# RWKV recurrence and feed-forward network in one kernel: state products in the mixing step, chunk 0 loaded in longer packets, new order tables

## The chip, the cores and the metric

The kernel runs on one core of a Trainium2 chip. The core has a matrix engine (TensorE, PE in the profile; its weight loads are listed as PEld), a vector engine (VectorE, DVE), an engine for activation functions (ScalarE, ACT), a general engine (GpSimd, POOL), and a synchronisation engine (SyncE, SP), which here issues nearly all DMAs. The engines run side by side, each through its own list of instructions in order, and wait for each other through semaphores. SBUF is the working memory of 128 partitions, PSUM the memory of eight banks into which TensorE writes. The metric is the time of one execution in microseconds, lower is better.

## The reference

For every batch entry b (4) and head h (8), a state matrix of 48 x 48 runs over 768 time steps; then all results go through a feed-forward network with a squared ReLU.

```python
B, H, S, D = r.shape                       # 4, 8, 768, 48
state = zeros((B, H, D, D))
for t in range(S):
    kt, vt, rt, wt = k[:, :, t], v[:, :, t], r[:, :, t], w[:, :, t]
    cur = einsum('bhd,bhe->bhde', u[None] * kt, vt)
    y[:, :, t] = einsum('bhd,bhde->bhe', rt, state + cur)
    state = wt[..., None] * state + einsum('bhd,bhe->bhde', kt, vt)
x = y.transpose(0, 2, 1, 3).reshape(B * S, H * D)     # 3072 x 384
h = maximum(x @ w_in, 0)                              # w_in 384 x 2048
out = (h * h) @ w_out                                 # w_out 2048 x 384
```

All arrays are fp32. The decays w lie between 0.80 and 0.95.

## The kernel before

**Units and chunks.** Time is cut into six chunks of 128 steps. One *unit* is one chunk c of one batch entry b, all eight heads; there are 24 units. Two heads share the partitions: head 2p stands on partitions 0 to 47, head 2p + 1 on 64 to 111 (J = 64, HP = 112), with p from 0 to 3 along the columns. Within a unit the recurrence becomes matrix products:

1. w, k and r of a unit arrive with time on the partitions (tile st). For chunks 1 to 5, DVE transposes blocks of 32 (L438) and 16 small DMAs spread them (L448), so that heads and channels stand on the partitions (tile pt). For chunk 0, TensorE does it: *turn* (L468), four transposes per tensor, into PSUM banks that are still free.
2. DVE forms the running products of w (scan, L484). ACT takes logarithm and exponential for the inverse (L491, L492), DVE multiplies: r~ = r times decay (rt, L495), and k~ by one Newton step (kn, L501, L502, L504).
3. beta is minus the sum over channels of r k u: two products on POOL (rk, L511, L513) and a sum on DVE (L514). ACT puts beta on the diagonals of two tiles Ms (diag, L521).
4. TensorE forms the scores of k~ and r~ (L532) into two banks, DVE copies the causal part over the diagonal tiles (mask, L536).
5. TensorE turns k~ back to time on the partitions (ktok, L544), ACT copies it to SBUF as Kt (L546).
6. The *mixing* step: products of the state with r~ (inter, L564) and of Ms with v (part, L572), in PSUM. ACT and DVE write the result as the feed-forward network's input x, in two fp32r parts hi and lo (L604, L605). In chunk 0, which has no state yet, the pair SPLIT is brought to its place by a copy ly and selection products (L586); later, small DMAs from tile x3 do that (L612).
7. The *state products* Kt with v (outer, L624): a step of its own with a bank of its own, then DVE adds them to the state (L632) and POOL multiplies by the decay of the chunk (L633). In chunk 0 DVE does the one product that is needed (L630). Chunk 5 needs none.

**Feed-forward.** The 2048 hidden columns are 16 steps f of 128. One step on the 512 columns of a chunk (4 batch entries x 128 steps of time) is: nine products into a bank hp (first, L653; three input tiles, each hi x hi, lo x hi, hi x lo), ReLU on ACT (L658), square on DVE (L659), hi part on ACT (L661), lo part on DVE (L662), then three products per batch entry that accumulate over all f in the banks ob0 to ob3 (second, L668). HALF = (6, 16, 0, ...) says that the first 6 steps of chunk 0 and all of chunk 1 run in two halves of two batch entries. The results leave through ACT copies and SP DMAs (L678, L682). For the last chunk, b = 1 and 3 are copied by DVE and go out through SP's queue, b = 0 and 2 by ACT through ACT's; b = 3 is copied half by DVE, half by ACT (L676, L680).

**Weights.** Both weight matrices arrive raw in eight groups g (two steps f each) and are split once into hi and lo parts in SBUF: two passes on ACT, three on DVE and one on POOL for each matrix of a group (split_w, L381). This lies beside chunks 0 and 1.

**PSUM.** Of the eight banks four are the accumulators ob, two are the pool hp and two the pool a. Scores, k~ turned back, mixing and state products all draw from the two a banks.

**What sets the order.** Every step is added to a planner (class Plan) with its engine, an estimated cost, a rank, and what it reads and writes. The planner runs a list schedule over estimated times (constants LAT, QUEUES, START, ...), takes among the steps that could start first the one of the lowest rank, hands out the tiles of the pools, and so writes one fixed order of instructions for each engine. The ranks come from the tables in class Ranks: one offset per kind of step, for chunk 0 (AT0), chunk 1 (AT1) and the others (AT), and for the weights and the feed-forward network. While PE would idle in the first 110 us by the plan, it gets *filler* transposes of the identity (L186, L712), which compute nothing. PE executes in this order: a step that is not ready holds up all behind it.

Of the kernel before, what the change touches and what calls it, by code (L numbers as in the profile page):

```python
# [35 lines left out]
class Plan:  # L36
# [156 lines left out]
class Ranks:  # L193
    AT = {'load': -139.75, 'z': 137.75, 'pt': -192, 'rk': -68, 'beta': -95.75, 'far': 178.75, 'v': 86, 'scan': 126.75, 'ln': -6.25, 'rt': -60.5, 'kn': 68.25, 'diag': -6.5, 'mt': -217.25, 'mask': 121.25, 'ktp': -306, 'kt': 263.5, 'mix': -111.5, 'x': 42.5, 'x3': -127.75, 'send': -288.5, 'dS': -95.75, 'S': -108.5}
    AT0 = {'load': -191.75, 'turn': -44.5, 'rk': 202.25, 'beta': -96, 'far': 179.75, 'v': -119, 'scan': -62, 'ln': 22, 'rt': -197.25, 'kn': -247.25, 'diag': -59.75, 'mt': -160.25, 'mask': -55.25, 'ktp': -67.75, 'kt': -39.75, 'mix': -207.25, 'x': -15.5, 'x3': -445.5, 'send': -140.25, 'dS': -172.75, 'S': -20.75}
    AT1 = {'load': -18.75, 'z': 292.25, 'pt': -54.25, 'rk': 265.5, 'beta': 219.25, 'far': 46.25, 'v': 45.75, 'scan': -1.25, 'ln': -41.5, 'rt': -120.5, 'kn': 3.25, 'diag': 57.75, 'mt': 3.5, 'mask': -138.5, 'ktp': 58, 'kt': 35, 'mix': -180.25, 'x': -185.5, 'x3': -144.25, 'send': -255.25, 'dS': -175.5, 'S': 98.75}
    U0 = (-54.25, -18, 58.5, 12)
    C1 = (5.5, 8.75, 72.25, 68.25)
    W0 = (-158.25, -38, -18.25, -1.25, 2.75, 4, 10, 16.25)
    WL = (17.5, -93.75, -2.75, -6.5, -3.75, 0.5, 9.25, 9)  # L200
    OFF = {'hp': 133.5, 'g': -8.25, 'ob': 69.5, 'os': 306}
    LAG = 74.5
# [18 lines left out]
RANKS = Ranks()  # L221
# [6 lines left out]
def kernel(  # L228
# [81 lines left out]
    st0 = [place(f"st0{i}", [128, 3, 2, H, J], F32, a) for i, a in enumerate((placed[f"ri{NG - 1}"], placed["x1"]))]  # L310
    for t in st0:
        V.memset(t[:, :, :, :, D:J], 1.0)
# [10 lines left out]
    P.pool("st0", [t.rearrange("s t b h x -> s (t b h x)") for t in st0])  # L323
# [92 lines left out]
    def attention(c, b, rank):  # L416
# [45 lines left out]
        if c == 0:  # L462
            home = (["o0", "o1", "o2"], ["o3", "hp", "hp"], ["o2", "o3", "a"], ["o2", "o3", "a"])[b]
            ps = {}
            for i, h in zip((0, 2, 1), (home[0], home[2], home[1])):
                ps[i] = Slot(h) if h in ("hp", "a") else ("ob", int(h[1]))

                def turn(i=i):  # L468
                    to = tl(ps[i]).rearrange("a (p s) -> a p s", p=NP)
                    pairs = st.tile.rearrange("s (t b p x) -> s t b p x", t=3, b=2, p=NP)[:, i, ui]  # L470
                    for p in range(NP):
                        T.transpose(out=to[:, p], in_=pairs[:, p], identity=ident)
# [119 lines left out]
        else:  # L592
# [3 lines left out]
            if ui == 0:  # L596
                d["x3"] = Slot("x3", n)
# [212 lines left out]
```

## Time and profile before

| | us |
|---|---|
| timed runs | 547.17, 552.87, 2872.64 (median 552.87) |
| profiled execution | 546.83 |
| its span, first to last instruction | 545.1 |
| PE busy / DVE / ACT / POOL | 525.9 / 361.2 / 289.9 / 103.0 |
| mean granted TensorE clock | 0.996 |

The profile gives for each engine the time in which an instruction of it was running. The sum over engines is far above the span because they overlap; what matters is which engine the others wait for in a given stretch. Busy PE time is an upper bound: matmuls are pipelined and their ends are modelled. "L653" is line 653 of the kernel printed above; "hp<-x,wi" says what is written and what is read; "SPq" and "ACTq" are issues of DMAs on those engines' queues; "in_w_dram" is an input in main memory.

### The profile page before, as it was taken

Reading aid. Unit: us, or ns where it says so; the run is one execution under the profiler, and the core shown is the slowest. Engines: PE = TensorE matmul, PEld = TensorE weight load, DVE = VectorE, ACT = ScalarE, POOL = GpSimd, SP = SyncE. Lnnn points to the kernel's source line nnn. Section 1 sums busy time; section 2 is a strip of 40 time slices with the busy share of each in tenths; the row PEclk is TensorE's granted clock in tenths of the full one; section 3 lists DMA queues with packets and bytes.
Section 4 is the critical chain, followed back from the end, with each engine's and each line's share of the span. In section 5 each row is a group of like instructions: output and inputs, shape, how many; then the busy total and the mean of one; then the engine's idle time right before and its main releaser. Section 6 shows DMA issues by size and latency. Waiting matters only on the chain.

```text
span 545.1 us, 10409 instructions
## 1 busy us (share of the span) xinstructions
PE 525.9 (96%) x3920; PEld 462.0 (85%) x3920; DVE 361.2 (66%) x672; ACT 289.9 (53%) x696; POOL 103.0 (19%) x119
## 2 busy tenths in 40 slices
PE   7888999999999999999999999999999999999994
PEld 6767988879999898888888888888888989999894
DVE  6899989989678595958779495976643233233241
ACT  2769886674854747466474756645333223233231
POOL 5344644532302020021202102020000000000000
PEclk9999999999999999999999999999999999999998
DMA  9999989158592776878375695954011000010001
GB/s 167 207 248 248 206 190 215 29 84 137 79 155 51 100 120 92 123 87 158 50 108 68 93 153 71 160 72 49 1 43 45 2 0 1 0 59 1 0 1 63
DMA packets 206584, 50.89 MB, mean 93 GB/s; under 512 B 196288, under 2 KB 201408, under 8 KB 206528
## 3 DMA queue, kind: packets, MB, share of 16 engines
q1 hardware_dynamic: 206096, 49.57, 52.7%
q8 instruction: 33, 0.54, 0.5%
q10 hardware_dynamic: 432, 0.59, 0.3%
q14 instruction: 23, 0.19, 0.1%
HBM read 31.65 MB, written 4.72 MB: 67 GB/s over the span
## 4 chain that ended last, share of the span: by engine, by line
PE 75%; DVE 7%; DMA 6%; SPq 5%; ACT 4%; issue 1%; DVEq 0%
PE hp L653 32%; PE ob L668 31%; PE a L572 4%; PE a L532 3%; DMA ri<-in_moe_w_in_dram 2%; SPq L429 2%; SPq L448 2%; PE a L564 2%; DMA st<-in_w_dram 1%; PE a L624 1%; ACT m L521 1%; PE a L544 1%; DVE st L438 1%; DMA v<-in_v_dram 1%; DVE g L662 1%
## 5 line engine op out<-in xcount | busy, mean ns | idle before, releaser
L653 PE MATMUL hp<-x,wi 128*128 128x512 f32 (+1 forms) x1062 | 220.5, 356 | 2.0 <-DVE g L662 1.8
L668 PE MATMUL ob<-wo,g 128*128 128x384 f32 x1152 | 221.4, 339 | 0.0
L668 PEld LDWEIGHTS ob<-wo,g 128*128 128x128 f32 x1152 | 198.5, 188 | 7.1 <-issue 2.0
L653 PEld LDWEIGHTS hp<-x,wi 128*128 128x128 f32 x1062 | 173.3, 188 | 32.7 <-DVE g L662 4.5
L658 ACT ACTIVATE t<-hp 128x512 f32<-128x512 f32 (+1 forms) x118 | 61.2, 519 | 119.8 <-PE ob L668 103.5
L659 DVE SCALAR_TENSOR_TENSOR hp<-hp,t 128x512 f32<-128x512 f32 (+1 forms) x118 | 70.1, 595 | 81.9 <-ACT t L658 80.8
L662 DVE TENSOR_TENSOR g<-hp,g 128x512 fp32r<-128x512 f32 (+1 forms) x118 | 68.8, 584 | 33.7 <-ACT g L661 31.7
L661 ACT CAST g<-hp 128x512 fp32r<-128x512 f32 (+1 forms) x118 | 59.6, 506 | 54.3 <-DVE hp L659 54.1
L521 ACT ACTIVATE m<-ident,beta 128x128 f32<-128x128 f32 x192 | 60.8, 393 | 5.0 <-DVE beta L514 4.8
L605 DVE SCALAR_TENSOR_TENSOR x<-a,x 112x128 fp32r<-112x128 f32 (+2 forms) x64 | 20.1, 344 | 31.4 <-ACT x L604 29.4
L511 POOL TENSOR_TENSOR st<-st 128x384 f32<-128x384 f32 x24 | 25.0, 1041 | 63.6 <-DVE st L438 62.5
L536 DVE COPY_PREDICATED m<-caus,a 128x512 f32<-128x512 uint8 x48 | 34.2, 731 | 4.1 <-PE a L532 4.1
L484 DVE TENSOR_TENSOR_SCAN pt<-pt,zero 112x128 f32<-112x128 f32 x80 | 29.6, 411 | 5.6 <-DMA x<-x 2.9
L572 PE MATMUL a<-m,v 128*48 128x128 f32 (+1 forms) x384 | 27.5, 278 | 1.9 <-DVE m L536 1.9
L532 PEld LDWEIGHTS a<-pt 48*128 48x128 f32 x384 | 23.6, 187 | 6.1 <-issue 2.7
L604 ACT ACTIVATE x<-a 112x128 fp32r<-112x128 f32 (+2 forms) x64 | 18.1, 322 | 19.6 <-PE a L572 18.1
L532 PE MATMUL a<-pt 48*128 48x128 f32 x384 | 28.2, 285 | 0.2
L491 ACT ACTIVATE m<-pt 112x512 f32<-112x512 f32 x24 | 15.2, 633 | 24.6 <-DVE pt L484 20.5
L438 DVE STREAM_TRANSPOSE st<-st 128x1152 f32<-128x1152 f32 x20 | 27.0, 1359 | 0.0
L513 POOL TENSOR_TENSOR st<-st,un 128x384 f32<-128x384 f32 x24 | 26.6, 1112 | 1.8
L572 PEld LDWEIGHTS a<-m,v 128*48 128x48 f32 (+1 forms) x384 | 20.2, 128 | 6.9 <-issue 4.4
L410 POOL TENSOR_TENSOR wi<-q,wi 128x768 fp32r<-128x768 f32 x8 | 16.1, 2018 | 43.3 <-ACT wi L409 24.3
(81 smaller groups left out, 394.9 us busy)
## 6 DMA issues: line engine op xcount, KB each, us to landing
pt<-st SPq DMA_DIRECT2D x80, 96.0 KB, 3.0
ro<-in_moe_w_out_dram SPq DMA_DIRECT2D x8, 768.0 KB, 6.6
v<-in_v_dram SPq DMA_DIRECT2D x24, 192.0 KB, 5.6
st<-in_w_dram SPq DMA_DIRECT2D x11, 384.0 KB, 4.2
st<-in_k_dram SPq DMA_DIRECT2D x11, 384.0 KB, 5.7
st<-in_r_dram SPq DMA_DIRECT2D x11, 384.0 KB, 6.4
pt<-st SPq DMA_DIRECT2D x80, 48.0 KB, 3.4
out_dram<-q SPq DMA_DIRECT2D x20, 192.0 KB, 3.2
```

The source lines that it names most:

```text
L438: V.transpose(out=zt[:, i].rearrange("a t p q i -> a t (p q) i"), in_=sv[:, :, i].rearrange("s t p q x -> s t (p q) x"))
L484: lambda p=p: V.tensor_tensor_scan(out=pt[:, 0, p], data0=src(0)[:, p], data1=zero.broadcast_to([HP, C]), initial=1.0, op0=ALU.mult, op1=A ...
L521: A.activation(mv(j)[:, p], ident, AF.Copy, scale=beta.tile[:, 2 * p + j:2 * p + j + 1])
L532: T.matmul(mts[j].tile.rearrange("s (p t) -> s p t", p=NP)[:, p], pt[js, 2, p], pt[js, 1, p], start=True, stop=True)
L536: lambda j=j: V.copy_predicated(out=mv(j), mask=caus.unsqueeze(1).broadcast_to([128, NP, C]), data=mts[j].tile.rearrange("s (p t) -> s p t ...
L572: T.matmul(spot(p)[to:to + n + D], vt.tile[:, o - n:o + D], mv(j)[:, p], start=(c == 0 and p == SPLIT), stop=True, skip_group_check=True)
L653: T.matmul(hp.tile[:, 0:n], wi[f][:, wl, kt], xT[:, kt, xl, xs], start=(m == 0), stop=(m == 3 * KT - 1))
L658: P.add("act", 0.5 if full else 0.28, rank("g"), lambda: A.activation(t(), h(), AF.Relu), r=[hp], w=[(g, 1)])
L659: P.add("dve", 0.61 if full else 0.33, rank("g"), lambda: V.scalar_tensor_tensor(out=h(), in0=h(), scalar=0.0, in1=t(), op0=ALU.max, op1=A ...
L661: P.add("act", 0.53 if full else 0.31, rank("g"), lambda: A.copy(out=hi(), in_=h()), r=[hp], w=[(g, 0)])
L662: P.add("dve", 0.61 if full else 0.33, rank("g"), lambda: V.tensor_tensor(out=lo(), in0=h(), in1=hi().bitcast(F32), op=ALU.subtract), r=[h ...
L668: T.matmul(obs[b][:, 0:DM], g.tile[0][:, gl, o:o + C], wo[f][:, wl], start=(f == 0 and m == 0), stop=(f == NF - 1 and m == 2))
```

## The change

- **State products.** For chunks 1 to 4, outer is called at the end of the mixing step and writes into columns 256 to 447 of the bank yb that holds two pairs of the mixing result. The step of its own and its bank are gone; the mixing step now also waits for Kt, and yb is kept until DVE has updated the state. In chunk 0 it stays a step of its own.
- **Loads of chunk 0.** w, k and r of each unit of chunk 0 come with (head, block of eight time steps) on the 128 partitions and 8 x 48 values, 1,536 bytes, in a row, one DMA per tensor and unit (12 instead of 9). The turn becomes 16 matmuls against columns of the identity, eight time steps by two heads of a pair, each writing 4 x 16 columns with a stride of eight.
- **r k u in chunk 0.** ACT writes -k into k~'s place, DVE multiplies it by r, and four small products with a column form of u (tile ut, made at the start from two small loads, a transpose and two copies) give beta in the bank that held w; ACT copies it out. The load of the row form of u goes from ACT's queue to SP's, after chunk 0's loads.
- **Squares of chunk 0.** ACT instead of DVE squares the ReLU result.
- **Last results.** All four go out on ACT's queue; b = 3 is copied by ACT in one piece, b = 1 still by DVE.
- **Planner.** New latencies, start and idle constants, some new costs, and new numbers in all rank tables.

The diff, cut to its core (the rank tables, all of which change, are left out but for one line):

```diff
-    LAT = {"pe": 0.2, "act": 0.1, "dve": 0.1, "pool": 0.1}
+    LAT = {"pe": 0.24, "act": 0.14, "dve": 0.14, "pool": 0.15}
...
-    LANES, RUNS, SLACK, START = 8, 2300, 2.0, 2.4
+    LANES, RUNS, SLACK, START = 8, 2300, 2.0, 1.4
...
-    IDLE = (110.0, 4.0, 0.3, 0.12)
+    IDLE = (110.0, 2.8, 0.3, 0.12)
...
-    OFF = {'hp': 133.5, 'g': -8.25, 'ob': 69.5, 'os': 306}
+    OFF = {'hp': 5.25, 'g': -342.5, 'ob': 16.25, 'os': -244}
...
-    st0 = [place(f"st0{i}", [128, 3, 2, H, J], F32, a) ...
+    TB = C // 16
+    st0 = [place(f"st0{i}", [128, 3, 2, TB * D + PC], F32, a) ...
     for t in st0:
-        V.memset(t[:, :, :, :, D:J], 1.0)
+        V.memset(t[:, :, :, TB * D:], 1.0)
+    ut = at.tile([HP, NP, 2], F32, name="ut")
+    V.memset(ut, 0.0)
...
-    nc.scalar.dma_start(out=un, in_=u.rearrange("h d -> (h d)").partition_broadcast(128))
-    G.tensor_scalar(out=un, in0=un, scalar1=-1.0, scalar2=None, op0=ALU.mult)
+    u8 = P.pools["m"][1][1][0:H, 0:HP]
+    V.memset(u8, 0.0)
+    for j in range(2):
+        nc.scalar.dma_start(out=u8[:, j * J:j * J + D], in_=u)
+    us = Slot("hp")
+    P.add("pe", 0.1, -300, lambda: T.transpose(out=us.tile[0:HP, 0:H], in_=u8, identity=ident[0:H, 0:H]), w=[us])
+    def columns():
+        for j in range(2):
+            js = slice(j * J, j * J + D)
+            A.copy(out=ut[js, :, j], in_=us.tile[js, j:H:2])
+    P.add("act", 0.3, -300, columns, r=[us], w=["ut"])
+    P.add("sp", 0.7, RANKS.unit(0, 3, "load") + 0.5, lambda: nc.sync.dma_start(out=un, ...
+    P.add("pool", 1.0, RANKS.unit(0, 3, "load") + 0.5, lambda: G.tensor_scalar(out=un, ...
...
-            for b0, m in ((b, 1), (b + 1, 1)) if (c, b) == (0, 0) else ((b, 2),):
+            for b0 in (b, b + 1) if c == 0 else ():
+                for i, src in ((0, w), (2, k), (1, r)):
+                    def load(i=i, src=src, b0=b0):
+                        nc.sync.dma_start(out=st.tile.rearrange("s (t b x) -> s t b x", t=3, b=2)[:, i, b0 - b, 0:TB * D],
+                                          in_=src[b0, :, ss, :].rearrange("h (a s) d -> h a (s d)", s=TB))
+                    P.add("sp", 0.65, rank("load") + b0 - b, load, w=[(st, b0 - b, i)], after=after, runs=128)
+            for b0, m in ((b, 2),) if c else ():
...
-                    to = tl(ps[i]).rearrange("a (p s) -> a p s", p=NP)
-                    pairs = st.tile.rearrange("s (t b p x) -> s t b p x", t=3, b=2, p=NP)[:, i, ui]
-                    for p in range(NP):
-                        T.transpose(out=to[:, p], in_=pairs[:, p], identity=ident)
-                P.add("pe", 0.5, rank("turn"), turn, r=[(st, ui, i)], w=[ps[i]])
+                    to = tl(ps[i]).rearrange("a (p x y) -> a p x y", p=NP, y=TB)
+                    rows = st.tile.rearrange("s (t b x) -> s t b x", t=3, b=2)[:, i, ui]
+                    pick = ident.rearrange("s (p j x) -> s p j x", p=NP, j=2)
+                    for y in range(TB):
+                        for j in range(2):
+                            n = (J, D)[j]
+                            T.matmul(to[j * J:j * J + n, :, :, y], rows[:, y * D:y * D + n], pick[:, :, j], start=True, stop=True, ...
+                P.add("pe", 1.0, rank("turn"), turn, r=[(st, ui, i)], w=[ps[i]], mode=3)
...
+        beta = Slot("beta")
+        if c == 0:
+            P.add("act", 0.53, rank("rk"), lambda: A.activation(pt[:, 2], src(2), AF.Copy, scale=-1.0), r=keys(2), w=[PT[2]])
+            P.add("dve", 0.62, rank("rk"), lambda: V.tensor_tensor(out=pt[:, 2], in0=pt[:, 2], in1=src(1), op=ALU.mult), r=keys(1), w=[PT[2]])
+            def sums():
+                for p in range(NP):
+                    T.matmul(tl(ps[0])[:, 2 * p:2 * p + 2], pt[:, 2, p], ut[:, p], start=True, stop=True, skip_group_check=True)
+            P.add("pe", 0.9, rank("beta"), sums, r=[PT[2], "ut"], w=[ps[0]])
+            P.add("act", 0.2, rank("beta"), lambda: A.copy(out=beta.tile, in_=tl(ps[0])[:, 0:H]), r=[ps[0]], w=[beta])
+        else:
...
+        if c < NC - 1:
+            dS = yb if c else Slot("a")
...
             def mix():
                 inter()
                 part((*TILES, SPLIT))()
+                if c < NC - 1:
+                    outer()
...
-            mixed = P.add("pe", 1.45, rank("mix"), mix, r=[vt, *Ms, ("S", b), *RK], w=[yb, far_yb], mode=3, claim=[x3])
+            P.add("pe", 2.0 if c < NC - 1 else 1.54, rank("mix"), mix, r=[vt, *Ms, ("S", b), *RK] + ([Kt] if c < NC - 1 else []), w=[yb, far_yb, (yb, "dS")], mode=3, claim=[x3])
...
-            P.add("pe", 0.5, rank("dS"), outer, r=[vt, Kt], w=[dS], mode=3, after=[mixed] if c else [])
+            if c == 0:
+                P.add("pe", 0.53, rank("dS"), outer, r=[vt, Kt], w=[dS], mode=3)
...
-        P.add("dve", 0.61 if full else 0.33, rank("g"), lambda: V.scalar_tensor_tensor(out=h(), in0=h(), scalar=0.0, in1=t(), op0=ALU.max, op1=ALU.mult),
-              r=[(g, 1)], w=[hp])
+        if c == 0:
+            P.add("act", 0.5 if full else 0.28, rank("g"), lambda: A.activation(h(), t(), AF.Square), r=[(g, 1)], w=[hp])
+        else:
+            P.add("dve", 0.61 if full else 0.33, rank("g"), lambda: V.scalar_tensor_tensor(out=h(), ...
...
-                if end and b % 2:
+                if end and b == 1:
...
-                if cut < DM:
-                    P.add("act", 0.25, rank("os"), lambda b=b, os_=os_, cut=cut: A.copy(out=os_.tile[:, cut:DM], ...
-                q_, e = ("actq", nc.scalar) if end and not b % 2 else ("sp", nc.sync)
+                q_, e = ("actq", nc.scalar) if end else ("sp", nc.sync)
```

More of the change, by code (lines that the diff above doesn't have):

```diff
@@ L196 @@
[L196 to L200, printed above, removed]
@@ L308 @@
     xTs = {0: at.tile([128, KT, 2, 512], F32R, name="x0"), 1: x1}
[L310 removed]
+    TB = C // 16
+    st0 = [place(f"st0{i}", [128, 3, 2, TB * D + PC], F32, a) for i, a in enumerate((placed[f"ri{NG - 1}"], placed["x1"]))]
     for t in st0:
[L312 removed]
+        V.memset(t[:, :, :, TB * D:], 1.0)
+    ut = at.tile([HP, NP, 2], F32, name="ut")
+    V.memset(ut, 0.0)
     obs = [ps_o.tile([128, 512], F32, name=f"ob{b}") for b in range(B)]
```

62 lines of the change are left out of this document (35 added, 27 removed).

## The prediction

> **What bounds the kernel now.** I read the page's engine shares first, then the busy times by stage, the filler transposes by stage, the chain of waits and the order of time at both ends. Stage rows give the window, its length, then PE, weight loads (PEld), DVE, ACT and POOL busy with instruction counts, the granted clock, the DMA share and GB/s.
>
> ```profile
> span 545.1 us, 10409 instructions
> PE 525.9 (96%) x3920; PEld 462.0 (85%) x3920; DVE 361.2 (66%) x672; ACT 289.9 (53%) x696; POOL 103.0 (19%) x119
> ```
> ```profile
> 0.00:15.00 15.00, 11.41 (x83) 9.68 (x84) 10.36 (x30) 4.86 (x10) 8.60 (x25) 1.00 0.91 173
> 15.00:30.00 15.00, 12.91 (x119) 10.72 (x119) 12.99 (x25) 10.72 (x28) 5.82 (x6) 1.00 1.17 214
> 30.00:45.00 15.00, 11.11 (x136) 8.96 (x138) 14.71 (x23) 11.47 (x30) 5.66 (x4) 1.00 1.14 229
> 45.00:60.00 15.00, 14.78 (x156) 13.16 (x153) 13.68 (x25) 12.55 (x33) 8.87 (x6) 1.00 1.07 281
> 60.00:75.00 15.00, 14.98 (x102) 14.25 (x102) 14.27 (x24) 14.76 (x39) 6.78 (x5) 1.00 0.81 134
> ...
> 90.00:135.00 45.00, 44.40 (x347) 38.16 (x349) 41.73 (x75) 27.85 (x63) 16.06 (x14) 1.00 0.63 97
> 135.00:375.00 240.00, 238.53 (x2007) 208.59 (x2001) 175.34 (x350) 143.82 (x386) 43.37 (x58) 1.00 0.68 101
> ...
> 465.00:480.00 15.00, 15.00 (x78) 13.77 (x77) 5.10 (x8) 5.53 (x10) 0.00 (x0) 1.00 0.08 26
> ```
>
> From 45 us on PE is busy 99% of the time (44.40 of 45, 238.53 of 240), so there only fewer PE instructions, or less switching between them, can save time. Before 45 us PE looks 76% busy, but the next rows, the same view for the filler transposes of L712 alone (PE, then PEld), say what that is worth.
>
> ```profile
> 0.00:15.00 15.00, 7.39 (x43) 6.36 (x44) 1.00 0.91 173
> 15.00:30.00 15.00, 6.53 (x55) 5.96 (x55) 1.00 1.17 214
> 30.00:45.00 15.00, 1.31 (x8) 0.84 (x8) 1.00 1.14 229
> ...
> 60.00:90.00 30.00, 2.01 (x14) 1.69 (x14) 1.00 0.94 192
> ```
>
> Fillers compute nothing: 7.39 + 6.53 + 1.31 = 15.2 us. With the idle PE time of 0 to 45 us (45 - 35.43 = 9.6 us), some 25 us pass there without PE work. That is all a better start can win. DVE carries that stage: its first scan starts at 6.73 us, and from 15 to 75 us it is busy 55.65 of 60. DMA is full as well (shares at or over 1 until 60 us), but DVE hardly waits for it after its first scan.
>
> **The change, part by part.** Everything is counted against the profiled execution, 546.8 us with a span of 545.1. The three timed runs (547.17, 552.87 and an outlier) have their median 1.1% above it; I forecast an execution like the profiled one.
>
> *Chunk 0's loads and turns.* The order of time at the start, start and length in us:
>
> ```profile
> 0.81 0.44 SPq L429 DMA_DIRECT2D st<-in_w_dram  x1
> 1.03 1.50 DVE L312 MEMSET st<- 128x768 f32 x2 [1.03 <-PEq L794]
> 6.06 0.63 PE L472 MATMUL ob<-ident,st 128*128 128x128 f32 x4 [0.65 <-DMA st<-in_w_dram]
> 6.73 1.37 DVE L484 TENSOR_TENSOR_SCAN pt<-ob,zero 112x128 f32<-112x128 f32 x4 [2.54 <-PE ob L472]
> 8.10 0.66 PE L472 MATMUL ob<-ident,st 128*128 128x128 f32 x4 [0.31 <-DMA st<-in_r_dram]
> 9.29 0.66 PE L472 MATMUL ob<-ident,st 128*128 128x128 f32 x4 [0.32 <-DMA st<-in_w_dram]
> ```
> ```profile
> un<-in_u_dram ACTq DMA_DIRECT2D x1, 192.0 KB, 4.5
> out_dram<-m ACTq DMA_DIRECT2D x2, 192.0 KB, 2.0
> out_dram<-m SPq DMA_DIRECT2D x2, 192.0 KB, 2.8
> ```
>
> The first w, 192 KB in 192-byte packets, is there at about 6.0 us, and the following loads come 9.29 - 8.10 = 1.19 us apart. Rows with 128 packets of 1,536 bytes land 2.0 us after issue on a quiet chip and 4.5 us in the crowd at the start. From an issue at 0.81 that puts w at 2.8 to 5.3 us, a gain of 0.7 to 3.2. The crowd itself goes (the 192 KB of u move from ACT's queue to SP's, behind other loads; two tiny loads of u stay), so I take 2.3. The DVE memsets shrink from 1,536 to 192 columns in all, which matters only because DVE must be free before the earlier scan.
>
> A turn becomes 16 matmuls of 64 columns for 4 transposes. The nearest row is the state products', 32 matmuls of 48 columns from 247.56 us, whose follower starts at 248.62 (quoted below): 16 take 0.53 us, at 64 columns 0.71, so 0.8 with the switch against 0.66. Only w's first turn lies ahead of the scan; the other eleven displace fillers (15.2 us of cover; uncovered they would cost 11 x 0.15 = 1.6 us). The first scan comes about 2.1 us earlier. The new turn writes every eighth column of a bank, which no row here does. The Trainium skill ("PSUM — Partial Sum Buffer", Specifications) says that non-contiguous patterns slow matmuls significantly; were that a doubling, my estimate is 0.7 us more per turn and a sum 1 us higher.
>
> *Products of r, k, u in chunk 0 and the squares.* Lines of DVE and ACT from 0 to 60 us, then the 512-column square over the whole run; the columns are count, busy us, mean ns:
>
> ```profile
> L501 DVE TENSOR_TENSOR pt<-pt,m 112x512 f32<-112x512 f32 x4 | 3.9, 984 | 0.1
> L514 DVE TENSOR_REDUCE beta<-st 128x8 f32<-128x384 f32 x5 | 2.7, 538 | 0.0
> L659 DVE SCALAR_TENSOR_TENSOR hp<-hp,t 128x256 f32<-128x256 f32 x6 | 2.5, 426 | 0.5 <-ACT t L658 0.3
> ```
> ```profile
> L491 ACT ACTIVATE m<-pt 112x512 f32<-112x512 f32 x4 | 2.5, 633 | 8.2 <-DVE pt L484 8.2
> L658 ACT ACTIVATE t<-hp 128x256 f32<-128x256 f32 x6 | 2.3, 384 | 5.0 <-PE hp L653 5.0
> ```
> ```profile
> L659 DVE SCALAR_TENSOR_TENSOR hp<-hp,t 128x512 f32<-128x512 f32 x74 | 51.5, 696 | 75.4 <-ACT t L658 74.6
> ```
>
> In chunk 0 DVE loses 12 x 0.43 + 10 x 0.70 = 12.1 us of squares, 2.5 of them before 60 us, and four reduces (2.2); it gains four multiplies of 512 columns, which I take at L659's 0.70 (2.8). POOL loses its eight products there. L501 takes 984 ns in this stage against 0.70 for another operation as wide, 4 x 0.28 = 1.1 us; if POOL's products are what stretches it, its neighbour L502 gains too, and I put the relief at 1.5 (bounds 0 and 2.2). DVE to 60 us: 2.1 earlier, and 2.5 + 2.2 + 1.5 - 2.8 = 3.4 less work: 5.5 us.
>
> ACT takes it over: four copies of k (at most 0.63 each), four of beta (8 columns, estimated at 0.2), and a square of 0.38 per half step: to 60 us 2.5 + 0.8 + 6 x 0.38 = 5.6 us on top of 39.6 (4.86 + 10.72 + 11.47 + 12.55). That is 45.2 us in the roughly 48 that are left if the stage shortens by 5.5 and ACT starts near 6 us. ACT, with 14.76 of 15 at 60 to 75 us already, becomes as tight as DVE, so I do not book the whole: **5.0 us** for the start, with 0 and 9 as bounds (nothing; or ACT's far checks are put off and the idle PE time shrinks too). The added PE work (four small products a unit, their transposes of u) stands under fillers. The sums wait for k's product and hold w's bank; the product in turn overwrites k's place and delays the later k~ of the same unit, with the unit's scores queued behind it on PE.
>
> From 60 to 135 us DVE loses the other 9.6 us of squares, but PE is nearly full: the fillers of 60:90 (2.0) and the 0.6 us idle at 90:135 are all that is to be had. I take **0.7**, bounds -1 (ACT late) and 2.5.
>
> *State products in the mixing step.* Order of time on PE in the middle:
>
> ```profile
> 245.77 1.86 PE L668 MATMUL ob<-wo,g 128*128 128x384 f32 x9
> 247.56 1.13 PE L624 MATMUL a<-v,m 128*64 128x48 f32 x32
> ```
> ```profile
> 516.19 4.18 PE ob L668 x24
> ```
>
> A product of L668 costs 4.18 / 24 = 0.174 us, nine 1.57; here they last 1.79 until the state products start, so stepping aside costs 0.22 us. Sixteen units (chunks 1 to 4), often two at a time: 8 to 16 such visits, 1.8 to 3.5 us, that the fused step saves but for its own change of shape. I take **1.5**, bounds 0 and 3.5. Bought with this: the fused step waits for the copy of k~ too, and its bank is kept until the state is updated.
>
> *The end.*
>
> ```profile
> 537.62 0.48 ACT L678 COPY m<-ob 128x384 f32<-128x384 f32 x1 [0.56 <-PE ob L668]
> 537.68 1.53 SPq L682 DMA_DIRECT2D out_dram<-m  x2
> 538.13 0.34 ACTq L682 DMA_DIRECT2D out_dram<-m  x1
> 538.53 0.32 ACT L680 COPY m<-ob 128x192 f32<-128x192 f32 x1 [0.44 <-DVE m L676]
> ```
>
> Now SP's last issue starts at about 538.9 and lands 2.8 (median of its two) later, 541.7. After the change ACT issues b = 2 until 538.47, copies b = 3 (0.48) and issues from 538.98, landing 2.0 later, 541.0. Both landings are medians of two, and a wait on the one queue that now carries all four issues could eat the gain: I take **1.2** rather than 0.7, since the last issue is the later one of SP's two, with bounds -0.5 and 1.7.
>
> *New orders.* Latencies and ranks cost nothing by themselves; what they move in the PE-bound part can be worth a microsecond either way, as no row shows it.
>
> Sum: 5.0 + 0.7 + 1.5 + 1.2 = 8.4; 546.8 - 8.4 = **538.4 us**.
>
> **The rivals.** (1) *The start gives all it has.* ACT's far checks are not needed early, so ACT need not bind: 9 + 2 + 2.5 + 1.2 = 14.7, **532 us**. For it: 25 us without PE work. Against it: 14.76 of 15 on ACT.
>
> (2) *The loads do not get faster.* The row 465:480 holds results in 1,536-byte packets: 26 GB/s at a share of 0.08, 325 GB/s for 16 busy engines, 0.6 us for 192 KB. Were only half of the engines used by such a load, it would take 1.2 us, just the spacing of now; units 1 to 3 arrive as late, and the start keeps only some 2 us of its gain, DVE still carrying it: 2 + 0 + 1.5 + 0.5 = 4, **543 us**. No row shows a transfer cut into 8 heads by 16 blocks. The Trainium skill ("DMA: Bandwidth & Descriptors", Why a DMA increments its semaphore by 16 and not by 1) has a DMA use the largest number of engines up to 16 that divides the slowest dimension on both sides, here 128 partitions and 8 heads, so 8; by that rule this case is the likelier one for the loads alone.
>
> (3) *Slower: the fused step waits.* PE runs in order, so a late copy of k~, or a bank held for a late state update, stops the feed-forward behind it.
>
> ```profile
> DVE S L632 <- PE a L624: 4.0, 5, 1.3
> ```
>
> The longest such wait now is 1.3 us, DVE's for the products. Turned around on PE in each of 16 units it is 21 us: 546.8 - 8.4 + 21 = **559 us**. It passes no change at 8.4 / 16 = 0.5 us per unit and 2% at 1.2. Against it: ACT is busy 143.82 of 240 us at 135:375, DVE 175.34, so both have room.
>
> **How the numbers follow.** Two per cent, what a measurement of this kernel can tell from no change, is 10.9 us: faster is below 535.9, slower above 557.7. Chances: forecast (535 to 541) 0.46, rival 1 0.26, rival 2 0.22, rival 3 0.06. The range runs from 530, with most of rival 1, to 548, with rival 2 and a gain eaten up; 0.8 or a little more lies within. Faster: rival 1 and a fifth of the forecast's own spread, 0.35; slower 0.06; within 2% 0.59.
>
> **What would show it.** Right: the first scan near 4.6 us; fillers before 45 us down from 15.2 towards 10; feed-forward products on PE about 5 us earlier; ACT the fuller engine from 15 to 75 us; no steps of state products between feed-forward groups; the last result landing on ACT's queue 2 us after issue. Wrong: loads still 1.2 us apart (rival 2), turns over 1.5 us, mixing steps preceded by PE waits for ACT or DVE (rival 3), or PE's fullness from 135 to 375 us under 98%.

## The result, and the profile after

The changed kernel takes 556.65 us (median of 10 runs, 554.33 to 560.27) beside 548.53 us for the kernel before (10 runs, one of them an outlier of 2872.64). The ratio is 1.0147, 95% interval 1.0119 to 1.0175: about 8 us slower, where 8.4 us faster was forecast. Its profiled execution took 555.8 us with a span of 554.1, against 546.8 and 545.1.

The first rows of the changed kernel's profile:

```profile
span 554.1 us, 11112 instructions
PE 535.4 (97%) x4280; PEld 478.8 (86%) x4280; DVE 353.6 (64%) x651; ACT 302.5 (55%) x728; POOL 94.8 (17%) x111
```

The busy times by stage of the changed kernel, columns as in the prediction:

```profile
0.00:15.00 15.00, 9.23 (x177) 8.98 (x179) 5.51 (x25) 3.97 (x10) 2.74 (x19) 1.00 0.54 167
15.00:30.00 15.00, 13.59 (x241) 13.02 (x238) 10.60 (x21) 11.07 (x35) 0.38 (x2) 0.77 0.93 240
30.00:45.00 15.00, 14.85 (x183) 12.79 (x178) 14.10 (x24) 10.74 (x23) 5.24 (x4) 1.00 1.04 253
45.00:60.00 15.00, 13.56 (x146) 11.00 (x146) 13.25 (x18) 11.95 (x30) 5.45 (x3) 1.00 1.00 244
...
135.00:375.00 240.00, 239.18 (x1976) 214.67 (x1975) 173.95 (x347) 139.59 (x367) 39.29 (x54) 1.00 0.59 101
```

In the middle PE is as full as it was (239.18 of 240). The loss arises in the first 60 us. DVE, which carried that stage at 12.99 of 15 from 15 to 30 us, now has 10.60 there and 5.51 before it; PE is the fuller engine from 15 to 30 us, and its granted clock is 0.77. From 30 to 45 us DVE is nearly full again (14.10). How much useful work this costs is read first from the feed-forward rows alone, the two lines of the same view for each kernel, first before (L653, then L668), then after (L693, then L711):

```profile
0.00:60.00 60.00, 7.41 (x56) 6.82 (x57) 1.00 1.07 224
...
0.00:60.00 60.00, 5.17 (x24) 4.02 (x24) 1.00 1.07 224
```
```profile
0.00:60.00 60.00, 4.00 (x27) 3.39 (x27) 0.94 0.88 226
...
0.00:60.00 60.00, 0.00 (x0) 0.00 (x0) 0.94 0.88 226
```

Before, 12.6 us of feed-forward were done by 60 us; after, 4.0. The last products, in the order of time before and after, end at 538.11 and at 546.76, 8.65 us apart, and from there to the end of the span it is 7.0 and 7.3 us:

```profile
536.73 1.38 PE L668 MATMUL ob<-wo,g 128*128 128x384 f32 x7
```
```profile
540.33 6.43 PE L711 MATMUL ob<-wo,g 128*128 128x384 f32 x36
```

That 8.6 us are missing at 60 us and 8.65 at the end is in part a coincidence, for feed-forward products are not all that is behind. By 60 us the kernel before has also done all state products of chunk 0 and turned all of its k~ back (L624, then L544); the changed kernel shows 0.00 us of both:

```profile
0.00:60.00 60.00, 2.57 (x64) 2.29 (x64) 1.00 1.07 224
0.00:60.00 60.00, 2.30 (x16) 1.73 (x16) 1.00 1.07 224
```

So it is some 13 us of PE behind at 60 us and makes up some 5 later. Fillers that it no longer runs after 60 us are 2.3 of these (2.28 us before, none after); for the rest no run tells the parts apart.

The order of time on PE in the changed kernel shows where the delay begins:

```profile
5.77 0.23 PE L359 MATMUL hp<-ident,m 8*112 8x8 f32 x1 [5.77 <-DMA m<-in_u_dram]
5.93 3.61 PE L752 MATMUL a<-ident 128*128 128x128 f32 x17
9.47 3.95 PE L497 MATMUL ob<-ident,st 128*64 128x64 f32 x128
13.36 1.05 PE L533 MATMUL ob<-ut,pt 112*128 112x2 f32 x8
```
```profile
10.68 1.36 DVE L509 TENSOR_TENSOR_SCAN pt<-ob,zero 112x128 f32<-112x128 f32 x4 [7.79 <-PE ob L497]
```

The transpose of u is the first instruction in PE's order, and it waits until 5.77 us for its tiny load. The 17 fillers that the order puts ahead of the first turn, meant to run while w is still on its way, come after it. The first turn starts at 9.47 us and the first scan at 10.68, where the prediction had 4.6 and the kernel before 6.73. The four turns that follow have 128 rows in the profile, 32 each, not 16.

### The profile page after: what moved, and what is told of

It is laid out like the page before. It is cut to its first block, busy times and chain, and to the rows that moved or that the text cites. A ratio compares the mean times of both kernels' runs of the same rounds, so it can differ in the third digit from the quotient of the medians.

```text
span 554.1 us, 11112 instructions
## 1 busy us (share of the span) xinstructions
PE 535.4 (97%) x4280; PEld 478.8 (86%) x4280; DVE 353.6 (64%) x651; ACT 302.5 (55%) x728; POOL 94.8 (17%) x111
## 4 chain that ended last, share of the span: by engine, by line
PE 73%; SPq 8%; DMA 7%; DVE 6%; ACT 3%; issue 1%; POOL 0%; DVEq 0%; ACTq 0%
PE ob L711 31%; PE hp L693 30%; SPq L469 5%; PE a L567 4%; PE a L607 4%; DMA ri<-in_moe_w_in_dram 4%; PE a L599 2%; DMA pt<-st 2%; DVE pt L509 1%; PE a L579 1%; PE a L624 1%; SPq L391 1%; DMA st<-in_r_dram 1%; ACT m L556 1%; DVE pt L520 1%
## 5 line engine op out<-in xcount | busy, mean ns | idle before, releaser
L693 PE MATMUL hp<-x,wi 128*128 128x512 f32 (+1 forms) x1062 | 224.2, 356 | 2.0 <-DVE g L705 1.9
L711 PE MATMUL ob<-wo,g 128*128 128x384 f32 x1152 | 224.9, 340 | 0.0
L711 PEld LDWEIGHTS ob<-wo,g 128*128 128x128 f32 x1152 | 200.5, 188 | 7.5
L693 PEld LDWEIGHTS hp<-x,wi 128*128 128x128 f32 x1062 | 174.2, 188 | 29.4 <-DVE g L705 3.9
L702 DVE SCALAR_TENSOR_TENSOR hp<-hp,t 128x512 f32<-128x512 f32 (+1 forms) x96 | 58.0, 604 | 93.6 <-ACT t L698 93.1
L705 DVE TENSOR_TENSOR g<-hp,g 128x512 fp32r<-128x512 f32 (+1 forms) x118 | 68.8, 583 | 31.7 <-ACT g L704 30.6
L567 PEld LDWEIGHTS a<-pt 48*128 48x128 f32 x384 | 25.3, 187 | 11.0 <-issue 3.6
L567 PE MATMUL a<-pt 48*128 48x128 f32 x384 | 30.8, 286 | 3.5 <-DVE pt L546 2.0
L538 POOL TENSOR_TENSOR st<-st 128x384 f32<-128x384 f32 x20 | 20.5, 1028 | 63.7 <-DVE st L459 63.7
L525 POOL COPY Ec<-pt 112x4 f32<-112x4 f32 x20 | 7.4, 370 | 106.9 <-DVE pt L509 96.9
L653 DVE SCALAR_TENSOR_TENSOR x<-a,x 112x128 fp32r<-112x128 f32 (+2 forms) x64 | 20.0, 341 | 7.9 <-ACT x L652 7.9
L425 POOL TENSOR_TENSOR wi<-q,wi 128x768 fp32r<-128x768 f32 x8 | 17.9, 2234 | 30.9 <-ACT wi L424 16.8
L540 POOL TENSOR_TENSOR st<-st,un 128x384 f32<-128x384 f32 x20 | 21.9, 1100 | 1.2
```

Source lines behind the costliest of these rows:

```text
L567: T.matmul(mts[j].tile.rearrange("s (p t) -> s p t", p=NP)[:, p], pt[js, 2, p], pt[js, 1, p], start=True, stop=True)
L693: T.matmul(hp.tile[:, 0:n], wi[f][:, wl, kt], xT[:, kt, xl, xs], start=(m == 0), stop=(m == 3 * KT - 1))
L702: P.add("dve", 0.61 if full else 0.33, rank("g"), lambda: V.scalar_tensor_tensor(out=h(), in0=h(), scalar=0.0, in1=t(), op0=ALU.max, op1=A ...
L705: P.add("dve", 0.61 if full else 0.33, rank("g"), lambda: V.tensor_tensor(out=lo(), in0=h(), in1=hi().bitcast(F32), op=ALU.subtract), r=[h ...
L711: T.matmul(obs[b][:, 0:DM], g.tile[0][:, gl, o:o + C], wo[f][:, wl], start=(f == 0 and m == 0), stop=(f == NF - 1 and m == 2))
```

## The experiments

Ratios are against the kernel before on the same chip. One per cent is 5.5 us.

**u behind the third turn.** Same order otherwise, the 17 fillers included.

```diff
-        for s in self.order():
+        todo = self.order()
+        late = [s for s in todo if getattr(s, "late", False)]   # u's transpose and its copies
+        ... put behind the third turn
+        for s in todo:
```

> The changed kernel, with only the transpose of u and its two copies on ACT issued behind the third turn; all else in the same order, the 17 fillers ahead of the first turn too. Theory A (u at the head of PE's order holds the first scan back, and the start never makes that up): the first turn starts near 5.5 us instead of 9.5, the first scan near 6.7 instead of 10.7, and the time falls by 3 to 4 us against the changed kernel (to a ratio near 1.008 against the kernel before). Theory B (the late loads of v hold the mixing, whatever the first scan does): the first scan comes as early, but unit 0's mixing stays near 40.8 us and the time falls by less than 1 us.

Measured: 1.0071 (1.0039 to 1.0104), 4.2 us under the changed kernel. Its order of time:

```profile
1.61 3.89 PE L758 MATMUL a<-ident 128*128 128x128 f32 x17 [1.61 <-POOL ident masks.py:199]
5.43 3.54 PE L503 MATMUL ob<-ident,st 128*64 128x64 f32 x96
7.16 1.37 DVE L515 TENSOR_TENSOR_SCAN pt<-ob,zero 112x128 f32<-112x128 f32 x4 [4.27 <-PE ob L503]
```

Theory A holds for half of the loss: w is there at 5.43 us at the latest, and the 4 us for which u and the fillers kept PE from it are not made up later.

**v earlier.** The loads of v for chunk 0 are issued at 25.6 to 30.6 us in the changed kernel; here they come behind the twelve loads of w, k and r.

```diff
+        v_load.early = c == 0      # and in run(): issued behind the twelfth load
```

> The changed kernel with the four loads of v for chunk 0 issued right behind the twelve loads of w, k and r; the rest of the order is as it was. Theory B: v is there by about 20 us, unit 0's mixing comes at 34 to 36 us instead of 40.8, the first feed-forward products near 46 instead of 52.5, and the time falls by 3 to 6 us. Theory A: v was late but not what was waited for; the mixing moves by less than 2 us and the time by less than 1.

Measured: 1.0147 (1.0083 to 1.0211), no difference from the changed kernel. Unit 0's mixing starts at 41.57 us instead of 40.81, though v is issued far earlier: it stands in PE's written order behind other units' turns and scores, and v is not what it waits for. Theory B falls.

**Blocks outermost: all 16 engines.**

```diff
-    in_=src[b0, :, ss, :].rearrange("h (a s) d -> h a (s d)", s=TB)
+    in_=src[b0, :, ss, :].rearrange("h (a s) d -> a h (s d)", s=TB)
...
-    pick = ident.rearrange("s (p j x) -> s p j x", p=NP, j=2)
+    pick = ident.rearrange("s (x p j) -> s p j x", p=NP, j=2)
```

> The changed kernel with the steps of chunk 0 spread over the partitions as block * 8 + head instead of head * 16 + block, and the identity's columns picked to match; packets, instructions and order are as they were. If the number of engines of such a load goes by the 8 heads as slowest dimension, this gives 16 engines: 16 flag packets a load, loads of one queue 0.6 to 0.7 us apart instead of 1.0, the twelve loads of chunk 0 in by about 11 us instead of 16. Theory A and B (PE's head or v set the start): the time stays within 1 us of the changed kernel. Theory C (the loads with half of the engines set the start): it falls by 2 to 5 us.

Measured: 1.0264 (1.0225 to 1.0304), 6.4 us over the changed kernel; none of the theories had that. The loads did get faster, but the edit changed a second thing: the operand that a turn moves through PE is now read with a stride of eight columns. Order of time on PE in this version, then the turns' rows (L497) from 0 to 62 us, first of the changed kernel, then of this version:

```profile
9.41 7.82 PE L497 MATMUL ob<-ident,st 128*64 128x64 f32 x128
```
```profile
0.00:62.00 62.00, 14.63 (x384) 13.89 (x384) 0.94 0.89 229
```
```profile
0.00:62.00 62.00, 23.73 (x384) 22.45 (x384) 0.98 0.97 240
```

A turn takes 7.82 / 4 = 1.96 us here, against 3.95 / 4 = 0.99. So it became an unplanned test of another kind: 9.1 us more of turns cost 6.4 us of time, 0.7 us for each (expectations further down reckon with 0.4). The prediction's cover of fillers would have hidden most of that.

**All three.** u late, blocks outermost with the strided operand, v earlier.

> The three edits together: u behind the third turn, 16 engines a load, v behind the twelve loads. If A and B are both right and the parts add up: 6 to 9 us under the changed kernel, that is level with the kernel before (ratio 0.995 to 1.003). If the order of the chunk 0 work by itself (which unit's step follows which, on DVE and ACT) is what costs the start: less than 3 us under it (ratio 1.009 or more).

Measured: 1.0152 (1.0113 to 1.0191). The parts do not add up as expected, since the slow turns (23.92 us of turns, as in the run before) take back what u gives.

**16 engines without the stride.** On top of u late, a copy of the identity with its columns in the turn's order.

```diff
+    pident = const.tile([128, 128], F32, name="pident")
+    A.copy(out=pident.rearrange("s (q x) -> s q x", x=16), in_=ident.rearrange("s (x q) -> s q x", x=16))
...
-    pick = ident.rearrange("s (p j x) -> s p j x", p=NP, j=2)
+    pick = pident.rearrange("s (p j x) -> s p j x", p=NP, j=2)
```

> The version with u behind the third turn, and the loads of chunk 0 with blocks outermost (16 engines), this time with a copy of the identity whose columns are already in the order that a turn picks, so that the operand of a turn is read without a stride again. If the stride of the operand is what doubled a turn from 0.49 to 0.98 us when the loads were cut the other way, the turns are back at 0.49 us. Theory C (half the engines hold the start back): all twelve loads are in by 11 us and the time falls by 2 to 4 us against u late alone. Theory A: the loads lie ahead of their need, and the time stays within 1 us.

Measured: 1.0063 (1.0028 to 1.0097), the same as u late alone. The turns are back at 1 us (64 rows, two of them, in 2.08 us from 12.16 us); the expectation's 0.49 and 0.98 us are for half a turn each. The stage row says that the engines are used:

```profile
0.00:15.00 15.00, 12.03 (x220) 11.36 (x220) 7.69 (x30) 6.46 (x18) 2.74 (x19) 1.00 0.84 219
```

The DMA share from 0 to 15 us is 0.84 at 219 GB/s, against 0.54 at 167 in the changed kernel. So the shares fit loads that use half of the engines in the changed kernel, and this costs nothing that shows: 0.4 us between the two ratios, with intervals of nearly 2 us to each side. Theory C's 2 to 4 us are not there, though 2 cannot be told from nothing this way.

**Fillers ahead of the first sums and scores.** On top of u late.

```diff
+            for name in ("sums", "scores"):
+                s = next(s for s in todo if s.fn.__name__ == name)
+                s.fill = (8, s.fill[1])
```

> The version with u behind the third turn, and on top of it 8 filler transposes ahead of the first step of sums and 8 ahead of the first scores, where TensorE stood idle for 0.9 us each time before its granted clock fell to 0.50 from 16.7 to 20.4 us. If short idle spells between sparse steps bring the clock down, the granted clock stays at 1.00 in that stage, the steps from 16.7 to 20.4 us take 1.5 to 1.9 us less, and the time falls by 1 to 2 us against the version with u late alone. If the clock goes by something else (the turns' own pattern), it falls all the same and the time stays within 0.7 us.

Measured: 1.0042 (1.0012 to 1.0072), 1.6 us under u late alone; the intervals overlap. The clock, in windows of 2 us of the changed kernel (the third number from the end), shows what it is about:

```profile
16.00:18.00 2.00, 0.91 (x18) 0.61 (x13) 2.00 (x6) 1.93 (x7) 0.19 (x1) 1.00 0.74 200
18.00:20.00 2.00, 1.68 (x17) 1.56 (x17) 1.17 (x3) 0.83 (x2) 0.00 (x0) 0.84 1.02 255
20.00:22.00 2.00, 2.00 (x27) 1.98 (x28) 0.87 (x3) 1.04 (x4) 0.00 (x0) 0.50 1.02 318
```

In the run with fillers the clock is 1.00 all through this stage; it fell later, from 48.8 to 55.6 us.

**The state products alone, in the old kernel.** The change's edits of the mixing step in the kernel before, with the old tables.

```diff
                 part((*TILES, SPLIT))()
+                if c < NC - 1:
+                    outer()
```

> The kernel before with the state products fused into the mixing step and nothing else of the change. The prediction had 1.5 us for it, 0 to 3.5 (ratio 0.997, 0.994 to 1.000). The trace of the changed kernel speaks for less: each entry into such a step saved, but 0.10 us per product where the two kinds of product meet, so a ratio of 1.000, 0.998 to 1.002.

Measured: 1.0080 (1.0044 to 1.0116). With the old tables the fusion costs 4 us, outside the prediction's bounds. The waits on PE from 60 to 540 us, first before, then here:

```profile
PE hp L653 <- DVE g L662: 1.8, 4, 1.0
```
```profile
PE hp L658 <- DVE g L667: 8.1, 9, 2.3
```

The feed-forward's first products wait 6 us more, in longer pieces, for DVE to be done with their bank. The likely reason, which no run singles out, is that the longer mixing step stands at places chosen for a shorter one: in the changed kernel, with other tables, this wait is 1.9 us.

**The squares alone, in the old kernel.**

```diff
+        if c == 0:
+            P.add("act", ..., lambda: A.activation(h(), t(), AF.Square), r=[(g, 1)], w=[hp])
```

> The kernel before with the squares of chunk 0 on ACT and nothing else of the change; the orders come out of the tables of before. The prediction counted 2.5 us less on DVE before 60 us and up to 0.7 us after: ratio 0.995 if DVE carries the start and ACT has room. If the ACT work makes up for it, or the order written for another split of the work fits badly, 1.000 to 1.008.

Measured: 1.0170 (1.0120 to 1.0220), 9 us slower. ACT is busy for all of 60 to 75 us, and PE waits 7.8 us for DVE's last step on its bank, which now follows ACT's square:

```profile
60.00:75.00 15.00, 14.26 (x96) 12.96 (x95) 13.84 (x21) 15.00 (x42) 6.97 (x5) 1.00 0.90 114
```
```profile
PE hp L653 <- DVE g L665: 7.8, 8, 2.3
```

Neither part helps the old kernel with its old tables. What they would do in an order of their own, these two runs cannot tell.

**Sums issued twice.** On top of u late; the result is the same.

```diff
-                for p in range(NP):
+                for p in (*range(NP), *range(NP)):
```

> The version with u behind the third turn, with each step of sums issued twice over (the second time with the same results): 3.8 us more of TensorE, all of it between ACT's copy of k and the score steps. If TensorE's added work in chunk 0 counts at the 0.4 us per us that slow turns cost, the time rises by 1.5 us against u late alone (ratio near 1.010). If it stands under fillers, as the prediction had it, nothing changes (ratio 1.006 to 1.008).

Measured: 1.0122 (1.0077 to 1.0166), 2.8 us over u late alone for 3.6 us more of sums (32 and 64 rows before 62 us, 4.11 and 7.68 us). The intervals overlap, and the mean granted clock of these executions is lower as well, 0.988 in the mean against 0.993 with u late. What such a difference of the clock is worth (last section) is about as large as the 2.8 us, so this run does not show by itself that the sums' time is uncovered.

**Turns issued twice, in the old kernel.** The counterpart in the old order.

```diff
-                    for p in range(NP):
+                    for p in (*range(NP), *range(NP)):
                         T.transpose(out=to[:, p], in_=pairs[:, p], identity=ident)
```

> The kernel before with each of its twelve turns issued twice (the second time with the same results): 6.5 us more of TensorE before 45 us, in the old order and with the old loads. The prediction let the turns' added time displace fillers, of which there are 15.2 us before 45 us: then ratio 1.000 to 1.002 (only w's first turn counts). If a turn lies on the chain from loads to scores and counts at about 0.4 us per us, as with the slow turns, the ratio is 1.004 to 1.007.

Measured: 1.0004 (0.9980 to 1.0027). The turns' rows from 0 to 62 us, before and here:

```profile
0.00:62.00 62.00, 7.65 (x48) 5.03 (x48) 1.00 1.07 227
```
```profile
0.00:62.00 62.00, 12.86 (x96) 10.29 (x96) 0.94 1.06 221
```

5.2 us more of turns cost 0.2 us, but part of the cost is masked. The mean granted clock is higher here, 0.993 against 0.990 over the timed executions, and at an equal clock this version is slower: at 0.988 its spans are 551.5 and 551.7 us, those of the kernel before on the same chip 548.6 to 549.6; at 0.996 they are 546.7 to 547.5 us against 545.2. So in the old order too the added turns cost some 2 us, and a higher clock pays for them. They displace no fillers either, for these are written into the order (15.2 us before, 15.6 here).

**Three edits.** u behind the first turn, 16 engines with the copied identity, fillers ahead of the first sums and scores.

> The changed kernel with three edits that keep its order: u's transpose and copies behind the first turn (behind the third they held ACT's first logarithm until 9.98 us), 16 engines per load with the copied identity, and the 16 fillers ahead of the first sums and scores. If u at the head and the fall of the clock make up the loss, it is level with the kernel before: ratio 0.998 to 1.002. If the turns and sums themselves carry what is left (8.5 and 4.4 us more of TensorE before 62 us, 0.4 us of time for each by the runs with slow turns), it stays 2 to 3 us behind: ratio 1.003 to 1.006.

Measured: 1.0029 (1.0001 to 1.0057): 6.5 of the 8 us are back, with the changed kernel's order. The feed-forward has 9.2 us done by 60 us (7.40 and 1.84), 3.3 behind the kernel before, and the span of the profiled execution, 548.5 us, is 3.4 longer.

**Four edits.** 17 more fillers ahead of and within the fourth unit's scores.

> The version with the three edits, and 8 and 9 more fillers ahead of and within the fourth unit's scores, where TensorE stood idle for 0.84 and 1.03 us just before its granted clock fell to 0.50 from 46.6 to 50.0 us. If the idle spells bring it down, the clock stays at 1.00 there, the steps of that stage take 1.7 us less, and the ratio falls from 1.003 to 0.999 to 1.001. If not, it stays at 1.003 and the clock falls somewhere between 40 and 60 us all the same.

Measured: 1.0067 (1.0045 to 1.0090), slower than without them, though the intervals overlap. The same kernel once more:

> The version with four edits once more, for its trace: it was slower than the one with three (1.0067 against 1.0029). If the 17 added fillers themselves lie in the chain, the fourth unit's scores end 1.5 to 3 us later than at 46.2 us and the clock stays at 1.00. If the clock fell all the same, it shows 0.50 for some us between 40 and 60.

This execution took 550.5 us, span 548.7. The clock stays at 1.00 in all of the first 60 us, where the version with three edits falls to about half:

```profile
46.00:48.00 2.00, 2.00 (x15) 1.88 (x11) 1.82 (x4) 1.41 (x2) 0.05 (x1) 0.63 1.04 271
48.00:50.00 2.00, 2.00 (x11) 1.42 (x11) 1.30 (x3) 1.31 (x4) 0.00 (x0) 0.52 0.89 233
```
```profile
46.00:48.00 2.00, 2.00 (x20) 1.56 (x17) 1.76 (x4) 1.21 (x3) 0.00 (x0) 1.00 0.99 261
48.00:50.00 2.00, 2.00 (x23) 1.70 (x22) 2.00 (x5) 1.66 (x6) 0.00 (x0) 1.00 1.00 223
```

The fourth unit's scores end at the same time (46.4 and 46.3 us), so the fillers are not in the way, and the first products after them take 1.32 us instead of 2.10. Yet the span is the same: PE's waits for DVE to free the feed-forward's banks after 60 us grow from 1.7 to 2.7 us. In the trace of the timed runs, with a span of 551.1 us and the clock at 1.00 all the same, they are 3.9 us. So what the clock gives back is, at least in part, lost again at those banks; why they come free later stays open. No version tried beats the kernel before.

## Why the prediction was wrong

**The start (5.0 us of gain): a loss of about 8.** Four of its steps failed.

*"Only w's first turn lies ahead of the scan."* The transpose of u lies ahead of it on PE, and was put "under fillers" with the other added PE work. It stood first in an engine that runs in order, waiting for a DMA that is issued outside the planner; behind it stood the fillers and then the turn. That is 4.2 us, half of the loss, as the run with u late shows. The question to ask was who is queued behind this instruction; the prediction asked it of the sums and the scores, not of u.

*"A turn becomes 16 matmuls of 64 columns."* It was priced at 0.8 us and takes 0.99 to 1.15 at full clock. Two of them, in the order of time of the changed kernel:

```profile
28.53 2.08 PE L497 MATMUL ob<-ident,st 128*64 128x64 f32 x64
```

The price per row was not too low (0.71 / 16 = 0.044 us forecast, 1.04 / 32 = 0.033 measured), but the count was: a matmul call of this kind has two rows in the profile, and a transpose one. The 32 rows of state products that served as a measure were 16 calls, for two units of eight. The turns grew from 7.65 to 14.63 us (part of it at half clock) and the sums came on top with 4.79 (the same), some 12 us of PE, where the prediction had 12 x 0.15 = 1.8 for the turns and no price for the sums. The sums also stand in the way of others: another unit's exponential stands behind the copy of beta in ACT's order, and that copy waits for sums at half clock:

```profile
20.96 0.17 ACT L535 COPY beta<-ob 128x8 f32<-128x8 f32 x1 [2.13 <-PE ob L533]
```

*"The other eleven displace fillers (15.2 us of cover)."* In sum they displaced none: fillers before 60 us take 15.61 us after (L752), 15.23 before (L712).

```profile
0.00:60.00 60.00, 15.61 (x111) 13.58 (x111) 0.94 0.88 226
0.00:60.00 60.00, 15.23 (x105) 13.16 (x105) 1.00 1.07 224
```

In the new order 9.1 us more of turns cost 6.4 us, clear of the noise. In the old one 5.2 us more cost 0.2, or some 2 at an equal clock, so the cover was thinner than booked there as well. The new tables put eleven of the twelve turns and three of the four sums between 9.5 and 31 us, nearly back to back, and the fillers elsewhere, as their rows by stage show (L752, columns PE and PEld):

```profile
15.00:30.00 15.00, 1.64 (x13) 1.40 (x13) 0.77 0.93 240
30.00:45.00 15.00, 7.84 (x62) 6.77 (x62) 1.00 1.04 253
```

From 15 to 30 us, where the turns are, the kernel before had 6.53 us of fillers. Cover is a property of the order that is run, and the prediction took it from the order that the change replaces. "Latencies and ranks cost nothing by themselves" was the sentence that let this through.

*DVE 5.5 us further on, ACT as tight as DVE.* DVE's relief came (43.5 us busy to 60 us instead of 51.7, though with less of the work done), but it could not start on it: 7.8 us of its first 10.7 pass in one wait for the first turn, as the first row of its waits from 0 to 60 us says (total, times, longest):

```profile
DVE pt L509 <- PE ob L497: 8.2, 2, 7.8
```

After 30 us DVE is as tight as before (14.10 of 15 from 30 to 45 us), and the chain that ended last runs over it from 42.2 to 49.5 us. ACT is not: it has 11.07, 10.74 and 11.95 of 15 in the three stages from 15 to 60 us.

The fall of the clock to 0.50 from 19.4 to 26.2 us was in no step. Fillers against it are worth 1.6 us in the version with u late, by ratios whose intervals overlap. What is left, about 1.6 us in the version with three edits (0.1 to 3.1 by its interval), is not settled. The added turns and sums are one candidate, by what the slow and the doubled turns cost. The new tables are the other: no run has the new steps with the old tables, so their own share was not measured.

**60 to 135 us (0.7) and the middle.** Not refuted, and not shown. PE is full, as before, but the changed kernel makes up some 5 us of work after 60 us, 2.3 of it by fillers that are gone, which the prediction had named. Which part of the change gives the rest no run tells.

**Fused state products (1.5, bounds 0 and 3.5).** A loss of 4 us with the old tables. In the new order no run singles the fusion out; a gain of its size can hide in what is made up after 60 us. More waiting on PE, as rival 3 had it, does appear with the old tables (8.1 us in place of 1.8), but not at the fused step: the rival named k~ and the bank, and the trace shows the feed-forward's buffers.

**The end (1.2).** No gain: 0.3 us lost, within the bounds. The order of time at the end of the changed kernel, and the last of the three issues alone:

```profile
546.27 1.00 ACT L720 COPY m<-ob 128x384 f32<-128x384 f32 x2 [0.56 <-PE ob L711]
546.86 1.36 ACTq L722 DMA_DIRECT2D out_dram<-m  x3
547.81 0.42 ACTq L722 DMA_DIRECT2D out_dram<-m  x1
```

The last copy ends at 546.27 + 1.00 = 547.27 us, but its issue starts only at 547.81, behind two others on the one queue: the wait that the prediction feared, 0.5 us. ACT's last issue ends at 548.22 us, 5.9 us ahead of the end of the span; SP's ended at 537.68 + 1.53 = 539.21 before, also 5.9 us ahead. So what follows the last issue takes as long on either queue, and the 0.8 us by which ACT's median landing was the shorter do not appear at the end; the changed kernel's profile gives no landing times.

**The rivals.** Rival 2's mechanism was right: loads with half of the engines, as the Trainium skill has it ("DMA: Bandwidth & Descriptors", Why a DMA increments its semaphore by 16 and not by 1). The trace agrees with that rule: a share of 0.54 with 8 heads as the slowest dimension, 0.84 with 16 blocks. Its price was not borne out: 0.4 us between two ratios whose intervals overlap, not some 3. Rival 1 had no part in it. A slower start was not among the cases at all; the chance of 0.06 for slower stood on the middle alone.

The rule of the Trainium skill that spoke against the new turn ("PSUM — Partial Sum Buffer", Specifications: non-contiguous patterns slow matmuls) is not borne out for the writes: with every eighth column written a row takes 1.04 / 32 = 0.033 us, and 1.13 / 32 = 0.035 in the state products' contiguous ones, though weight loads fill the turns' time too (PEld 13.89 of 14.63 us). It is a stride in the operand read from SBUF that doubled a turn.

## What to carry to other kernels

An instruction that waits for a load at the head of an engine's order holds up all that is queued behind it, however small it is: put it behind the first work that is ready, or let the planner know its load. Before work is booked as hidden, look whether its cover still stands beside it in the order that will be run; a change of the order tables can take the cover away and leave every step as it was. When two counts agree, as 8.6 and 8.65 us do here, look for what neither counts. Count rows, not calls: one call can be two instructions, and a row taken as a measure must be counted the same way.

## What the runs showed of the hardware

A turn whose moving operand is read with a stride of eight fp32 columns takes 1.96 us, and 1.04 with the same columns copied next to each other; the strided writes to PSUM cost nothing visible.

The granted clock fell to 0.50 within the work in most traces of the study (12 of 15), for 3.4 or 6.8 us each time and at places that differ from kernel to kernel. The Trainium skill ("TensorE: Matmul & The Clock Gate", Part 1) has it fall after an idle window of about 3.4 us. The traces differ on the idle time: in the changed kernel it fell at 19.4 us after two spells of 0.7 us, and with the same spells it can fall or stay. In the kernel before PE is idle for 0.89 and 1.05 us from 40.6 us on, in the one with its turns issued twice for 0.88 and 1.06 us from 43.3 us on. The first stayed at 1.00, the second fell:

```profile
46.00:48.00 2.00, 2.00 (x20) 1.86 (x20) 0.99 (x2) 0.98 (x4) 1.83 (x1) 1.00 1.07 287
```
```profile
46.00:48.00 2.00, 2.00 (x16) 1.43 (x14) 2.00 (x4) 2.00 (x7) 0.68 (x1) 0.50 1.00 254
```

So one profiled execution can be several us off the median for this alone, and a stage of it should be read together with its clock. In the kernel before, on one chip, four executions with a mean clock of 0.988 have spans of 548.6 to 549.6 us, and one with 0.996 has 545.2: about 0.5 us for each 0.001. At the very start the rows run at half speed although the clock is given as 1.00: with u late, 17 fillers take 3.89 us from 1.61 us on, 0.23 each; in the changed kernel 45 of them take 5.13 us from 32 us on, 0.11 each.
